# A second level of the seven-product scheme for two products of the first layer

## The chip, the cores and the metric

The kernel runs on one core of one Trainium2 chip. The metric is the device time of one execution in microseconds, the median over runs. The core has TensorE (PE; its weight loads are shown apart as PEld), VectorE (DVE), ScalarE (ACT), GpSimd (POOL) and SyncE (SP, which here issues nearly all DMAs). DVE, ACT and PE can reach PSUM, the eight banks that hold the results of matmuls; POOL works in SBUF.

## The reference: attention over pooled keys, then two layers

```python
def _attn_ref(q, k, v):                       # q, k, v: (8, 8, 576, 64)
    k_p = k.reshape(B, H, Sp, pool, D).mean(axis=3)     # pool = 8, Sp = 72
    v_p = v.reshape(B, H, Sp, pool, D).mean(axis=3)
    scores = scale * np.matmul(q, k_p.transpose(0, 1, 3, 2))
    scores = scores - np.max(scores, axis=-1, keepdims=True)
    attn = np.exp(scores)
    attn = attn / (np.sum(attn, axis=-1, keepdims=True) + 1e-09)
    return np.matmul(attn, v_p)

def _moe_ref(x, w_in, w_out, alpha):          # x: (4608, 512), w_in: (512, 2048)
    h = x @ w_in
    s = np.sin(alpha * h)
    g = h + s * s / (alpha + 1e-09)
    return g @ w_out                          # w_out: (2048, 512)
```

The rows of x are the attention's output, batch by batch, with the heads side by side. All is fp32.

## The kernel before

**The first layer.** `hidden(u, extra)` runs once for each of nine units of 512 rows of x. It uses a scheme for products of 2 x 2 blocks that needs seven block products instead of eight: x is halved in its rows and in its 512 features, `w_in` in its features and in its 2048 outputs. `self.A[1..7]` hold the seven weight blocks (plain ones and sums), `bt[u][:, 0..3]` the four sums of x's blocks. A unit has four groups, J = 0 to 3, of 2 x 128 outputs in each half. A group has seven slots, k = 0 to 6, with one block product each, in the order 1, 5, 6, 2, 7, 3, 4. A block product is four matmuls: 128 x 128 weights, 256 moving columns, two row blocks jj by two halves kk of the contraction. So a unit has 28 slots, numbered 7 J + k.

**The banks.** A group uses four PSUM banks (b1, b6, b5, b7) out of five that rotate. Sums of the scheme are made in place: ACT copies b1 into b6 and product 6 accumulates there; ACT copies b6 into b7, and products 7 and later 4 accumulate there; product 2 accumulates into b1, product 3 into b6. Product 5 is copied to SBUF as `p5`. The four results are b1 (after product 2), b7 + p5 (after product 7, called g11 here for `g[:, 1, :, 1]`), b6 + p5 (after product 3, g01) and b7 after product 4. DVE makes the two additions of p5. ACT applies the sine and then the square, and DVE adds the squares to h in `finish`. `store_g` sends g to a buffer in DRAM. Product 4 may only be issued once g11 has been read out of b7.

**The order.** The order of every engine's instructions is the order in which the code emits them; nothing reorders it. Each slot emits first what the slot before left (`self.left`), then the `extra` work of the slot, then its product:

```python
            def left2(G=G, Q=before, late=late):
                ...
                nc.scalar.copy(out=G.b7[:], in_=G.b6[:])
                G.p5 = self.tp.tile([P, JW, TH], F32, name="p5")
                nc.scalar.copy(out=G.p5[:], in_=G.b5[:])
            def left3(G=G):
                sin(G, 0, 0, G.b1)
                square(G, 0, 0)
            def left4(G=G):
                add(G.g[:, 1, :, 1], G.b7[:], G.p5[:])
```

`left2` is emitted at the start of slot k = 3, `left3` at k = 4, `left4` at k = 5. Q is the group before; its last squares (`squares(Q)`) are emitted at k = 1, its `finish` at k = 2.

**The attention beside it.** `carry(u)` places the attention of batch u + 1 into unit u as extra work. For units 1 to 6: scores at slots 3 and 5 (`two_scores`, PE in banks 5 to 7 and one rotating bank, with the shifts by the maximum on DVE, the last at slot 6), `load_v` at 6, the exps on ACT at slots 8, 9, 10, 10, the norms (DVE reduction and reciprocal, POOL product) at 9, 10, 11, 12, the DVE transposes `turn` at 12, 12, 13, 13, 16 DMAs `move` on SP at 14, `all_values` at 25 (PE, then copies into x by ACT), the next keys' transposes at 26. `turn_q` prepares q of batch u + 2 at slots 22 to 25: in parts 0 and 1 DVE transposes q into the tile `tr`, which `move` reads before that, and parts 2 and 3 send it on by DMA. q lies in two buffers of one pool (`qp`, `name="q"`), and `load_q(u + 3)` is at slot 7.

**The second layer** (`outputs`, L1112) comes after the first; it already uses the scheme at two levels, with 144 moving columns.

Of the kernel before, what the change touches and what calls it, by code (L numbers as in the profile page):

```python
# [13 lines left out]
F32 = mybir.dt.float32  # L14
AX = mybir.AxisListType.X
AF = mybir.ActivationFunctionType
# [3 lines left out]
P = 128  # L20
POOL = 8
TH = 256
# [18 lines left out]
class Kernel:  # L41
# [31 lines left out]
        self.load_q_rest(b)  # L73

    def new_q(self, b):
        self.qm[b] = self.qp.tile([P, 5 * self.H * self.D], F32, name="q")

    def load_q_heads(self, b, h0, h1, dma=None):
        main = self.q_views(self.qm[b])[0]
# [3 lines left out]
    def pairs_q(self, b, tiles):  # L83

        nc = self.nc
        if 0 in tiles:
            self.raw = self.q_views(self.qm[b])
            self.qm[b] = self.qp.tile([P, 5 * self.H * self.D], F32, name="q")
        x = self.qm[b][:].rearrange("p (t h e d) -> p t e h d", t=5, e=2, d=self.D)
        for t in tiles:  # L90
            n = P if t < 4 else 64
            raw = self.raw[0][:, :, t, :] if t < 4 else self.raw[1]
            nc.scalar.copy(out=x[:n, t], in_=raw.rearrange("p (e h) d -> p e h d", e=2))
# [135 lines left out]
    def attention(self, b):  # L229
# [22 lines left out]
        def q_t(i, copy=nc.scalar.copy):  # L252

            n = rows[i]
            x = self.qm[b][:n].rearrange("p (t hp x) -> p t hp x", t=5, hp=NP)[:, i]
            if b not in self.qt:
                self.qt[b] = self.qt_view(self.qp.tile([P, 5 * H * D], F32, name="q"))
            ps = self.abank([P, NP, P])
            for hp in range(NP):
                nc.tensor.transpose(ps[:, hp, :n], x[:, hp], self.ident[:n, :n])  # L260
            copy(out=self.qt_tiles(b)[:, i, :, :n], in_=ps[:, :, :n])
# [100 lines left out]
        def q_head(hp):  # L362

            if hp == 0:
                self.qt[b] = self.qt_view(self.qp.tile([P, 5 * H * D], F32, name="q"))
            main = self.q_views(self.qm[b])[0]
            ps = self.psum([P, 4, P], 1 + hp % 2)
            for e in range(2):
                for tp in range(2):
                    nc.tensor.transpose(ps[:, 2 * e + tp, :], main[:, 2 * hp + e, 2 * tp:2 * tp + 2, :].rearrange("p t d -> p (t d)"), self.ident[:])  # L370
            nc.scalar.copy(out=self.qt_tiles(b)[:, hp], in_=ps)
# [365 lines left out]
    def abank(self, shape):  # L737

        self.aturn = (self.aturn + 1) % 3
        return self.psum(shape, 5 + self.aturn)  # L740

    def sums_of_x(self, u, n):

        nc = self.nc
        if u not in self.bt:
            self.bt[u] = self.home(3, [P, 4, 2, TH])
        xT, bt = self.xT[u], self.bt[u]
        B = lambda i, j: xT[:, 2 * i:2 * i + 2, j * TH:(j + 1) * TH]
        o, x, y = ((0, B(0, 1), B(0, 0)), (1, B(1, 1), bt[:, 0]), (2, B(1, 1), B(0, 1)), (3, B(1, 0), bt[:, 1]))[n]
        nc.vector.tensor_tensor(out=bt[:, o], in0=x, in1=y, op=OP.subtract)  # L750

    def hidden(self, u, extra):

        nc = self.nc
        bank = lambda: self.bank([P, JW, TH])
        add = lambda o, x, y: nc.vector.tensor_tensor(out=o, in0=x, in1=y, op=OP.add)  # L756

        for slot in range(7 * self.NJ):
            J, k = divmod(slot, 7)
            for f in self.left:  # L760
                f()
            for f in extra[slot]:
                f()
            if k == 0:
                before = self.group
                G = self.group = SimpleNamespace(
                    u=u, J=J, b1=bank(), g=self.hp.tile([P, 2, JW, 2, TH], F32, name="h"),
                    s=self.hp.tile([P, 2, JW, 2, TH], F32, name="s", bufs=1))
            xT, bt = self.xT[u], self.bt[u]
            B = lambda i, j: xT[:, 2 * i:2 * i + 2, j * TH:(j + 1) * TH]  # L770

            def product(p, ps, start):
                x = {1: B(0, 0), 2: B(1, 0), 3: B(1, 1), 4: bt[:, 3], 5: bt[:, 0], 6: bt[:, 1], 7: bt[:, 2]}[p]
                for jj in range(JW):
                    f = J * JW + jj
                    for kk in range(2):
                        nc.tensor.matmul(ps[:, jj, :], self.A[p][:, kk, f * P:(f + 1) * P], x[:, kk, :],  # L777
                                         start=(start and jj == 0 and kk == 0), stop=(kk == 1), skip_group_check=True)

            def sin(G, i, j, src):  # L780
                for jj in range(JW):
                    f = i * self.K2 // 2 + G.J * JW + jj
                    nc.scalar.activation(out=G.s[:, i, jj, j, :], in_=src[:, jj], func=AF.Sin, scale=self.al[:, f:f + 1])  # L783

            def square(G, i, js):

                for jj in range(JW):
                    f = i * self.K2 // 2 + G.J * JW + jj
                    x = G.s[:, i, jj, js, :]
                    nc.scalar.activation(out=x, in_=x, func=AF.Square, scale=self.c[:, f:f + 1])  # L790

            early = lambda G: G.J == (0 if G.u else 1)

            def squares(G):
                if not early(G):
                    square(G, 0, 1)
                square(G, 1, slice(0, 2))

            self.squares = squares

            def left0(G=G, Q=before):
                G.b6 = bank()
                nc.scalar.copy(out=G.b6[:], in_=G.b1[:])  # L803
                if Q:
                    squares(Q)

            def left1(G=G, Q=before):
                if Q:
                    self.finish(Q)

            late = G.J == 0 and 0 < u < self.B - 1

            def left2(G=G, Q=before, late=late):
                if Q and not late:
                    self.store_g(Q)
                G.b7 = bank()
                nc.scalar.copy(out=G.b7[:], in_=G.b6[:])
                G.p5 = self.tp.tile([P, JW, TH], F32, name="p5")
                nc.scalar.copy(out=G.p5[:], in_=G.b5[:])

            def left3(G=G):
                sin(G, 0, 0, G.b1)
                square(G, 0, 0)

            def left4(G=G):
                add(G.g[:, 1, :, 1], G.b7[:], G.p5[:])

            def left5(G=G, Q=before, late=late):
                if late:
                    self.store_g(Q)  # L830
                add(G.g[:, 0, :, 1], G.b6[:], G.p5[:])
                sin(G, 1, 1, G.g[:, 1, :, 1])
                add(G.g[:, 0, :, 0], G.b1[:], G.s[:, 0, :, 0])

            def left6(G=G):
                sin(G, 0, 1, G.g[:, 0, :, 1])
                if early(G):
                    square(G, 0, 1)
                sin(G, 1, 0, G.b7)

            self.left = [(left0, left1, left2, left3, left4, left5, left6)[k]]
            if k == 1:
                G.b5 = bank()
            p = (1, 5, 6, 2, 7, 3, 4)[k]
            product(p, getattr(G, {1: "b1", 5: "b5", 6: "b6", 2: "b1", 7: "b7", 3: "b6", 4: "b7"}[p]), k < 2)

    def finish(self, Q):
        add = lambda o, x, y: self.nc.vector.tensor_tensor(out=o, in0=x, in1=y, op=OP.add)  # L848
# [8 lines left out]

    def end_hidden(self):
        nc, Q = self.nc, self.group
        for f in self.left:  # L860
            f()
        self.squares(Q)
        self.finish(Q)
        self.store_g(Q)

# [90 lines left out]
    def carry(self, u):  # L956
# [6 lines left out]
        if u == 0:  # L963
# [36 lines left out]
            at(20, A.move, (3,), nc.scalar)  # L1000
            at(26, A.all_values)
            at(9, self.load_q, 2)
            at(14, self.load_q, 3)
            for e in range(2):
                at(12, self.load_k, 2, e)
                at(17, lambda e=e: self.pool_k[e]())
# [5 lines left out]
        if 0 < u < last:  # L1012
# [3 lines left out]
            at(6, A.two_shifts)  # L1016
            for i in range(4):
                at((8, 9, 10, 10)[i], A.exp, i)
                at((9, 10, 11, 12)[i], A.norm, i)
                at((12, 12, 13, 13)[i], A.turn, i)  # L1020
            at(14, A.move, range(4))
            at(6, self.load_v, b)
# [5 lines left out]
            at(25, A.all_values)  # L1028
            if b < last:
                at(26, self.att[b + 1].k_t)  # L1030
            if u + 3 <= last:
                at(7, self.load_q, u + 3)
            turn = 22
        elif u:
            turn = None
# [218 lines left out]
    def run(self):  # L1254
        nc, tc = self.nc, self.tc
        pool = lambda s, n, b, **kw: s.enter_context(tc.tile_pool(name=n, bufs=b, **kw))
        with ExitStack() as top:
# [10 lines left out]
            with ExitStack() as one:  # L1268
# [5 lines left out]
                att = one.enter_context(ExitStack())  # L1274
                cb = pool(att, "cb", 1)
                self.kvp = pool(att, "kv", 2)
                self.qp = pool(att, "qp", 2)
                self.ap = pool(att, "ap", 1)
                self.sm = pool(att, "sm", 3)
                one.enter_context(tc.manual_schedule(engines=engines))  # L1280
# [6 lines left out]
                self.twos = cb.tile([P, 64], F32, name="twos")  # L1287
                self.eights = cb.tile([64, 32], F32, name="eights")
                self.mask = cb.tile([P, 4], F32, name="mask")
                self.last = cb.tile([64, 640], F32, name="last")  # L1290
                self.last_t = cb.tile([P, 5, 64], F32, name="last_t")
                nc.vector.tensor_reduce(out=self.twos[:], in_=ident[:].rearrange("p (m k) -> p m k", k=2), axis=AX, op=OP.add)
                x = ident[:64, :64].rearrange("p (m k) -> p m k", k=8)
# [1 line left out]
                    nc.vector.tensor_reduce(out=self.eights[:, 8 * s:8 * s + 8], in_=x, axis=AX, op=OP.add)  # L1295
                nc.vector.tensor_reduce(out=self.mask[:], in_=ident[:].rearrange("p (g s k) -> p s g k", s=4, k=8), axis=mybir.AxisListType.XY, op=OP.add)
                self.qm, self.qt, self.kp, self.vp, self.pair, self.pool_k = {}, {}, {}, {}, {}, {}
                self.bt, self.left, self.group, self.turn = {}, [], None, 2
                self.R = {}
                self.first_batch()  # L1300
                for u in range(self.NU):
                    x = self.carry(u)
                    if u == self.B - 1:
# [61 lines left out]
```

## Time and profile before

| | us |
|---|---|
| median of 3 runs | 911.84 |
| the runs | 911.52 to 913.13 |
| the profiled execution | 911.39 |
| its span, first to last instruction | 909.6 |
| unit 2, PE busy of 144.06 to 199.65 | 55.59 |
| ACT busy in the same stretch | 39.21 |
| DVE busy in the same stretch | 36.06 |
| ACT busy of 157.7 to 172 (14.3 us, J = 1) | 12.88 |
| DVE busy of 157.7 to 172 | 11.62 |

The mean granted TensorE clock is 0.999. A matmul of fp32 shows as two records. In a timeline row the columns are start, duration, engine, line, operation, result and sources, shape, count, and in brackets the idle time of the engine before it with what ended it. In a row of several instructions the duration runs from the start of the first to the end of the last, and successive instructions of an engine overlap a little: a row of two ACT squares takes 0.90 us, though one takes 0.50.

### The profile page before, as it was taken

To read this page: it belongs to the slowest core of one execution; us is meant where nothing else is said; L and a number is where in the kernel's file an instruction comes from. 1 tells how busy PE (TensorE), PEld (TensorE's weight loads), DVE (VectorE), ACT (ScalarE), POOL (GpSimd) and SP (SyncE) were. 2 spreads that over 40 slices of the span, in tenths; PEclk is the share of its full clock that TensorE was granted. 3 is DMA by queue.
4 is the path that set the end of the run, shared out by engine and by line. 5 is a ranking of instruction groups with operands and counts; after the bars stand their busy time and mean duration, and the time that the engine had idled before them with its cause. 6 is when DMAs were issued, how large, how long until landed. Compare 5 with 4: busy or idle time off the path is not lost.

```text
span 909.6 us, 17730 instructions
## 1 busy us (share of the span) xinstructions
PE 899.5 (99%) x7002; PEld 814.6 (90%) x7002; DVE 664.0 (73%) x1006; ACT 436.1 (48%) x998; POOL 170.9 (19%) x159
## 2 busy tenths in 40 slices
PE   8999999999999999999999999999999999999997
PEld 5787888888888888888888899999999999999997
DVE  6675766758567574663466899979788888889895
ACT  5696775867658676686876621111111111111111
POOL 4785350703408044140000000000000000000000
PEclk9999999999999999999999999999999999999999
DMA  9985867758577575538227247161618162534401
GB/s 253 249 252 153 213 166 193 198 173 224 162 190 192 165 199 171 148 109 307 76 84 249 93 117 226 37 216 37 225 27 222 41 188 73 170 92 128 134 14 40
DMA packets 134794, 141.12 MB, mean 155 GB/s; under 512 B 49896, under 2 KB 103288, under 8 KB 134712
## 3 DMA queue, kind: packets, MB, share of 16 engines
q1 hardware_dynamic: 132536, 138.03, 53.2%
q10 hardware_dynamic: 2176, 1.97, 0.8%
q8 instruction: 55, 0.90, 0.4%
q14 instruction: 27, 0.22, 0.1%
HBM read 75.37 MB, written 47.19 MB: 135 GB/s over the span
## 4 chain that ended last, share of the span: by engine, by line
PE 88%; DMA 4%; POOL 2%; DVE 2%; SPq 1%; ACT 1%; issue 1%; ACTq 0%; POOLq 0%; DVEq 0%
PE PS L1112 42%; PE PS L777 41%; DMA kvin<-in_v_dram 2%; PE PS L575 2%; PE PS L287 2%; SPq L642 1%; POOL kvin L118 1%; PE PS L588 1%; DMA a<-in_moe_w_in_dram 1%; POOL ex L344 1%; DMA h<-in_k_dram 1%; ACT s L790 0%; POOL as L648 0%; DVE h L848 0%; ACT s L783 0%
## 5 line engine op out<-in xcount | busy, mean ns | idle before, releaser
L777 PE MATMUL PS<-home,a 128*128 128x256 f32 x1152 | 264.3, 381 | 1.2 <-ACT home L502 0.8
L777 PEld LDWEIGHTS PS<-home,a 128*128 128x128 f32 x1152 | 216.6, 190 | 37.4 <-issue 4.6
L777 PE MATMUL PS<-home,as 128*128 128x256 f32 x864 | 200.3, 381 | 0.3 <-ACT PS L803 0.2
L777 PEld LDWEIGHTS PS<-home,as 128*128 128x128 f32 x864 | 162.5, 190 | 23.9 <-issue 1.0
L1112 PE MATMUL PS<-s,wb 128*128 128x144 f32 x896 | 119.4, 286 | 0.4 <-ACT PS L1232 0.4
L1112 PEld LDWEIGHTS PS<-s,wb 128*128 128x128 f32 x896 | 113.7, 190 | 0.7 <-ACT PS L1232 0.6
L118 POOL TENSOR_TENSOR kvin<-kvin 96x768 f32<-96x768 f32 (+3 forms) x42 | 74.8, 1782 | 196.8 <-DMA kvin<-in_v_dram 195.2
L790 ACT ACTIVATE s<-s,c 128x256 f32<-128x256 f32 (+1 forms) x216 | 110.0, 573 | 0.0
L756 DVE TENSOR_TENSOR h<-PS,p 128x512 f32<-128x512 f32 x72 | 49.2, 684 | 79.5 <-PE PS L777 42.2
L783 ACT ACTIVATE s<-h,al 128x256 f32<-128x256 f32 x144 | 65.1, 503 | 56.5 <-DVE h L756 52.7
L1232 ACT COPY PS<-PS 128x144 f32<-128x144 f32 x56 | 14.7, 263 | 145.7 <-PE PS L1112 144.3
L783 ACT ACTIVATE s<-PS,al 128x256 f32<-128x256 f32 x144 | 60.0, 468 | 32.1 <-PE PS L777 18.4
L1112 PE MATMUL PS<-r,wb 128*128 128x144 f32 x512 | 73.2, 286 | 0.0
L1112 PE MATMUL PS<-s,a 128*128 128x144 f32 x512 | 73.2, 286 | 0.0
L848 DVE TENSOR_TENSOR h<-PS,s 128x512 f32<-128x512 f32 x36 | 24.6, 684 | 63.7 <-ACT s L790 63.7
L1112 PEld LDWEIGHTS PS<-r,wb 128*128 128x128 f32 x512 | 67.1, 190 | 0.1
L1112 PEld LDWEIGHTS PS<-s,a 128*128 128x128 f32 x512 | 67.1, 190 | 0.0
L1251 ACT COPY PS<-PS 128x144 f32<-128x144 f32 x56 | 14.7, 263 | 88.4 <-PE PS L1112 88.4
L1112 PE MATMUL PS<-s,we 128*128 128x144 f32 x384 | 54.9, 286 | 0.0
L1112 PE MATMUL PS<-x,wb 128*128 128x144 f32 x384 | 54.9, 286 | 0.0
L1112 PEld LDWEIGHTS PS<-s,we 128*128 128x128 f32 x384 | 50.4, 190 | 0.1
L1112 PEld LDWEIGHTS PS<-x,wb 128*128 128x128 f32 x384 | 50.3, 190 | 0.0
(187 smaller groups left out, 1185.1 us busy)
## 6 DMA issues: line engine op xcount, KB each, us to landing
g_bridge<-h SPq DMA_DIRECT2D x72, 512.0 KB
r<-g_bridge SPq DMA_DIRECT2D x31, 1152.0 KB
out_dram<-o SPq DMA_DIRECT2D x124, 72.0 KB
kvin<-in_k_dram SPq DMA_DIRECT2D x14, 576.0 KB
q<-in_q_dram SPq DMA_DIRECT2D x7, 1024.0 KB
kvin<-in_v_dram SPq DMA_DIRECT2D x14, 512.0 KB
aM<-tr SPq DMA_DIRECT2D x54, 92.0 KB
aM<-tr SPq DMA_DIRECT2D x54, 88.0 KB
```

The costliest lines, as they stand in the source:

```text
L118: self.nc.gpsimd.tensor_tensor(out=t[..., 0:w] if w > D else out, in0=t[..., 0:w], in1=t[..., w:2 * w], op=OP.add)
L287: nc.tensor.matmul(ps[e][r0 + r:r0 + r + q.shape[-1], h, :], q[s], kb[s, hp, :], start=True, stop=True)
L344: nc.gpsimd.tensor_tensor(out=E(i), in0=E(i), in1=sm.unsqueeze(2).to_broadcast([P, n, Sp]), op=OP.mult)
L575: nc.tensor.matmul(o[r:r + 64], w, x, start=start and i < 2, stop=False, skip_group_check=True)
L756: add = lambda o, x, y: nc.vector.tensor_tensor(out=o, in0=x, in1=y, op=OP.add)
L777: nc.tensor.matmul(ps[:, jj, :], self.A[p][:, kk, f * P:(f + 1) * P], x[:, kk, :], start=(start and jj == 0 and kk == 0), stop=(kk == 1), ...
L783: nc.scalar.activation(out=G.s[:, i, jj, j, :], in_=src[:, jj], func=AF.Sin, scale=self.al[:, f:f + 1])
L790: nc.scalar.activation(out=x, in_=x, func=AF.Square, scale=self.c[:, f:f + 1])
L848: add = lambda o, x, y: self.nc.vector.tensor_tensor(out=o, in0=x, in1=y, op=OP.add)
L1112: nc.tensor.matmul(out, W[:, J // 2, J % 2, :], A[:, J, :], start=(start and J == 0), stop=(J == self.NJ - 1), skip_group_check=True)
L1232: nc.scalar.copy(out=x1[:, 0, :], in_=x0[:, 1, :])
L1251: nc.scalar.copy(out=x1[:, 1, :], in_=x1[:, 0, :])
```

## The change

Three groups (J = 1 to 3) of units 1 to 6 compute product 5 by seven products of a second level, and group 3 of these units also product 1. The 256 rows and the 256 features are halved again, and so are the two output blocks jj; each inner product is one matmul of 128 x 128 weights and 128 moving columns. `inner_w_in` makes the inner weights once, at slot 23 of unit 0, on POOL, in the first of the two q buffers, which holds no q afterwards. `inner_x` makes the inner sums of x for each unit, at slot 2, on POOL. The inner scheme works in place in the product's own bank; it needs one more bank (7 for product 5, 6 for product 1), three ACT copies and one DVE addition.

In these groups slot 1 has no product 5. Its inner products are spread: a at k = 0, b at k = 1 (k = 2 for J = 3), d at k = 3, e at k = 4 (k = 3 for J = 3). The second half of product 4 is issued after a and product 1 of the next group. The copy of p5 follows e, `finish` and the store of the group before move from k = 2 and 3 to k = 3 after d, and the squares of the group before are partly at k = 3. For J = 3, the inner products of product 1 are issued within products 3 and 4 of J = 2. The first norm goes from slot 9 to 10, and q of batch u + 2 (no longer u + 3) is loaded at slot 7. Groups in which nothing is split keep their order, now written out slot by slot.

```diff
 def new_q(self, b):
-        self.qm[b] = self.qp.tile([P, 5 * self.H * self.D], F32, name="q")
+        self.qm[b] = self.q_tile(b > 1)
+
+    def q_tile(self, i):
+        return self.qp.tile([P, 5 * self.H * self.D], F32, name=f"q{int(i)}")
...
+    def inner_w_in(self):
+        w = self.q_tile(0)[:]
...
+            self.sums(((s1, L(1, 0), L(1, 1), OP.add), (s2, s1, L(0, 0), OP.subtract), (s3, L(0, 0), L(1, 0), OP.subtract), (s4, L(0, 1), s2, OP.subtract)))
+            self.W2[p] = J0, {1: L(0, 0), 2: L(0, 1), 3: s4, 4: L(1, 1), 5: s1, 6: s2, 7: s3}
+
+    def inner_x(self, u):
...
+            self.sums(((t1, R(0, 1), R(0, 0), OP.subtract), (t2, R(1, 1), t1, OP.subtract), (t3, R(1, 1), R(0, 1), OP.subtract), (t4, R(1, 0), t2, OP.subtract)))
+            self.X2[p] = {1: R(0, 0), 2: R(1, 0), 3: R(1, 1), 4: t4, 5: t1, 6: t2, 7: t3}
+
+    def sums(self, steps):
+        for o, x, y, op in steps:
+            self.nc.gpsimd.tensor_tensor(out=o, in0=x, in1=y, op=op)
...
     def hidden(self, u, extra):
...
+        two = 0 < u < self.B - 1
...
             if k == 0:
...
+                if Q and not N:
+                    self.last_sines(Q, 2 if not inner else 0)
+                extras()
+                G = self.group = N or begin(J)
+                self.next = None
+                if G.i5:
+                    G.i5.a()
+                if G.i1:
+                    self.last_sines(Q, 0)
+                else:
+                    product(G, 1, G.b1, True)
+                    if G.i5:
+                        product(Q, 4, Q.b7, part=(2, 3))
+            elif k == 1:
+                if not G.i1:
+                    copy(G.b6[:], G.b1[:])
+                if G.i5 and not G.i1:
+                    self.last_sines(Q, 1)
+                    G.i5.b()
+                if Q and not G.i1:
+                    squares(Q, 0)
+                    if not G.i5:
+                        squares(Q, 1)
+                extras()
+                if not G.i5:
+                    product(G, 5, G.b5, True)
+            elif k == 2:
+                if Q and not G.i5:
+                    self.finish(Q)
+                extras()
+                if G.i1:
+                    product(G, 6, G.b6, part=(0, 1))
+                    G.i5.b()
+                    self.last_sines(Q, 1)
+                    product(G, 6, G.b6, part=(2, 3))
+                else:
+                    product(G, 6, G.b6)
+            elif k == 3:
...
+                copy(G.b7[:], G.b6[:])
+                G.p5 = self.tp.tile([P, JW, TH], F32, name="p5")
+                if not G.i5:
+                    copy(G.p5[:], G.b5[:])
+                else:
+                    if G.i1:
+                        squares(Q, 0)
+                    squares(Q, 1)
+                    G.i5.d()
+                    self.finish(Q)
+                    self.store_g(Q)
+                extras()
+                product(G, 2, G.b1)
+                if G.i1:
+                    G.i5.e()
+                    copy(G.p5[:], G.b5[:])
+            elif k == 4:
                 sin(G, 0, 0, G.b1)
+                if not G.i5:
+                    square(G, 0, 0)
+                extras()
+                product(G, 7, G.b7, part=(0, 1))
+                if G.i5:
+                    if not G.i1:
+                        G.i5.e()
+                        copy(G.p5[:], G.b5[:])
+                    square(G, 0, 0)
+                product(G, 7, G.b7, part=(2, 3))
+            elif k == 5:
                 add(G.g[:, 1, :, 1], G.b7[:], G.p5[:])
+                extras()
+                N = None
+                if two and J + 1 == 3:
+                    N = self.next = begin(J + 1)
+                    N.i1.a()
+                product(G, 3, G.b6, part=(0, 1))
+                if N:
+                    N.i1.b()
+                product(G, 3, G.b6, part=(2, 3))
+            else:
...
+                if not N:
+                    last()
+                    extras()
+                    product(G, 4, G.b7, part=(0, 1))
+                    if not (two and J < 3):
+                        product(G, 4, G.b7, part=(2, 3))
+                else:
+                    product(G, 4, G.b7, part=(0,))
+                    N.i1.d()
+                    last()
+                    product(G, 4, G.b7, part=(1, 2))
+                    N.i1.e()
+                    copy(N.b6[:], N.b1[:])
+                    extras()
+                    product(G, 4, G.b7, part=(3,))
...
+    def inner_product(self, G, p, ps, y):
...
+        def a():
+            products((1, 5), (y[:, 0], y[:, 1]), True)
+            nc.scalar.copy(out=f[:, 0], in_=y[:, 0:1].to_broadcast([P, 2, P]))
+            m5[p] = self.sm.tile([P, 1, P], F32, name=f"m{p}", bufs=1)
+            nc.scalar.copy(out=m5[p][:], in_=y[:, 1:2])
+
+        def b():
+            products((6, 2), (c[1], c[0]))
+            nc.scalar.copy(out=c[2], in_=c[1])
+
+        def d():
+            products((7,), (c[2],))
+            x = ps.rearrange("p i t -> p (i t)")[:, P:3 * P].rearrange("p (i t) -> p i t", i=2)
+            nc.vector.tensor_tensor(out=f[:, :, 1], in0=x, in1=m5[p][:].to_broadcast([P, 2, P]), op=OP.add)
+
+        def e():
+            products((3, 4), (c[1], c[2]))
...
-            at(14, self.load_q, 3)
+            at(23, self.inner_w_in)
...
-                at((9, 10, 11, 12)[i], A.norm, i)
+                at((10, 10, 11, 12)[i], A.norm, i)
...
-            if u + 3 <= last:
-                at(7, self.load_q, u + 3)
+            if 2 < u + 2 <= last:
+                at(7, self.load_q, u + 2)
+            at(2, self.inner_x, u)
...
-                self.qp = pool(att, "qp", 2)
+                self.qp = pool(att, "qp", 1)
```

`last_sines(Q, 0)` emits the sine (0, 1) of the group before, part 1 its sine (1, 0), part 2 both; `begin` takes the four banks and makes the inner objects i5 and i1.

## The prediction

> **What bounds the kernel now.** I read the page's busy times first, then its chain that ended last, then the timeline of one unit (unit 2, from 144.06 us) engine by engine.
>
> ```profile
> span 909.6 us, 17730 instructions
> PE 899.5 (99%) x7002; PEld 814.6 (90%) x7002; DVE 664.0 (73%) x1006; ACT 436.1 (48%) x998; POOL 170.9 (19%) x159
> PE 88%; DMA 4%; POOL 2%; DVE 2%; SPq 1%; ACT 1%; issue 1%; ACTq 0%; POOLq 0%; DVEq 0%
> PE PS L1112 42%; PE PS L777 41%; DMA kvin<-in_v_dram 2%; PE PS L575 2%; PE PS L287 2%; SPq L642 1%; POOL kvin L118 1%; PE PS L588 1%; DMA a<-in_moe_w_in_dram 1%; POOL ex L344 1%; DMA h<-in_k_dram 1%; ACT s L790 0%; POOL as L648 0%; DVE h L848 0%; ACT s L783 0%
> ```
>
> TensorE is the bound, and the products of the first layer (L777) carry 41% of the chain. So removed TensorE time counts in full, and so does every new wait of TensorE. ACT at 48% looks harmless; that share is a mean, and the place to look is group J=1, where the attention's four exps lie.
>
> ```profile
> 157.72 3.62 PE L777 MATMUL PS<-home,a 128*128 128x256 f32 x16
> 161.18 3.62 PE L777 MATMUL PS<-home,as 128*128 128x256 f32 x16
> 164.63 3.66 PE L777 MATMUL PS<-home,a 128*128 128x256 f32 x16
> ...
> 161.86 1.33 ACT L790 ACTIVATE s<-s,c 128x512 f32<-128x512 f32 x2
> 163.21 1.28 ACT L336 ACT_TABLE_LOAD   x1
> 164.51 1.26 ACT L336 ACTIVATE ex<-ex 128x576 f32<-128x576 f32 x2
> 165.67 0.58 ACT L817 COPY PS<-PS 128x512 f32<-128x512 f32 x1
> 166.19 0.57 ACT L819 COPY p<-PS 128x512 f32<-128x512 f32 x1
> 166.66 1.49 ACT L336 ACTIVATE ex<-ex 128x576 f32<-128x576 f32 x2
> 168.17 1.28 ACT L783 ACT_TABLE_LOAD   x1
> 169.47 0.84 ACT L783 ACTIVATE s<-PS,al 128x256 f32<-128x256 f32 x2
> ...
> 168.33 0.69 DVE L756 TENSOR_TENSOR h<-PS,p 128x512 f32<-128x512 f32 x1
> ...
> 175.07 10.08 SPq L488 DMA_DIRECT2D aM<-tr  x16
> 187.08 2.37 DVE L210 STREAM_TRANSPOSE tr<-q 128x1024 f32<-128x1024 f32 x2 [3.65 <-DMA aM<-tr]
> ```
>
> The reader should see three things. TensorE runs a product pair in 161.18 - 157.72 = 3.46 us, without a gap. ACT is full from 161.4 to 172: the copy of b7 ends at 166.25 where product 7 starts at 166.36, and the copy of p5 (166.19) stands before exps 2 and 3, the table load and the next sine (169.47). DVE's transposes of q at 187.08 wait for the 16 moves, which SP needs 10.08 us to issue.
>
> **What the Trainium skill says.** "TensorE: Matmul & The Clock Gate", section "LDWEIGHTS (loading the stationary operand)", gives columns / 1.2 ns: 107 ns for 128 columns. The trace agrees: four loads in 0.52 us at 11.04 (L353), the last 0.22 long, are about 0.10 apart. The same page, "Architectural detail: the array is 16× 32×32, not 1× 128×128", says that ACT and DVE take their work strictly in order; every timeline row above follows the order in which the code issues. "ScalarE: Activation LUTs", "What ACT_TABLE_LOAD costs", gives 1283 ns plus about 1380 ns of drain; the trace shows 1.28 us and the exp 0.02 later, so no drain is paid here. The same page, "Table sets: the hidden batching unit", has cheap functions in every set; whether Square runs without a load between two exps no row of before shows, and the change puts it there.
>
> **The change part by part.** Its own execution is 911.39 us for a span of 909.6, 0.45 under the median of 911.84.
>
> *Removed from TensorE.* 6 units x (3 + 1) = 24 products. Before: 4 matmuls, two records each, 8 x 3.45/16 = 8 x 0.2156 = 1.725 us. After: 7 matmuls of 128 columns. The nearest row is a transpose of 128 columns (15.99, eight in 1.04 us, the last 0.276 long): (1.04 - 0.276)/7 = 0.109 apart, equal to the load's pace. 14 x 0.109 = 1.526; saved 0.199, x24 = 4.8 us. Upper bound for a record: the second layer's 144 columns, 374.48/3057 = 0.1225, which leaves 0.01 a product, 0.2 us in all. I take 0.109: 0.80 us saved per unit.
>
> *Added to ACT.* For each inner product three PSUM copies of 256, 128 and 128 columns. Between L1209 (288: 0.383) and L1232 (144: 0.263) they take about 0.36 and 0.25, and advance the queue by 0.27, 0.16 and 0.16. DVE gets an addition of 256 (about 0.42); POOL eight small operations per unit at slot 2 (0.455 each, the 128x128 row of L118), while it waits for v (195.2 us over 7 waits), so nothing; with that cover gone, 3.6 us of POOL ahead of the pooling of v. The weights' sums fall into POOL's idle time after 80.4 us. The q loads start one unit later, slot 7 for a use at slot 22, 26 us ahead, on an SP queue whose v load lands in 9.4 us: nothing, at worst a few tenths at slot 22. Units 0, 7 and 8 keep their order.
>
> *Moved, J=1.* The copy of p5 now stands behind the sine of product 2 (slot 11), and so behind all four exps and both table loads. Times from t0 = 157.72 (end of product 3 of J=0), with the advances of the trace. TensorE: half of product 4 to 0.86, m1 and m5 to 1.30, product 1 to 3.03, the other half to 3.89, m6 and m2 to 4.33, product 6 to 6.06, m7 to 6.28, product 2 to 8.00, half of product 7, m3 and m4, the rest of 7, to 10.17, product 3 to 11.89. ACT: sine and squares from 0.93 to 2.54, the two copies to 2.97, b6 (waits for product 1, +0.20) 3.23 to 3.72, sine of b7 4.09 to 4.83, copy to 5.08, table load 6.38, two exps 7.54, b7 copy ends 8.11 (product 7 waits 0.15), squares 9.27, two exps 10.78, table load 12.08, sine 12.81, p5 ends 13.4. Then DVE must add b7 + p5 (0.69) before product 4 may accumulate into b7. DVE itself: finish waits for the squares (9.4), takes 0.6 + 1.35, then three of the norms at 0.92 each to about 14.1, and only then that addition, to 14.8. Product 4 is due at 12.05. Stall: 2.7. If DVE were free it would still be 13.4 + 0.75 - 12.05 = 2.1.
>
> *J=2.* On DVE, two turns (1.6) and the last norm (1.18) still stand before the addition of b6 + p5; it ends near 17.9, the sine after it 18.8, the copy that m6 needs 19.2. TensorE is there at 14.8 + 0.86 + 0.44 + 1.73 + 0.86 = 18.7: 0.7 lost, and 0.2 on the b6 copy behind it. ACT has no exps here and catches up.
>
> *J=3.* The last turn ends 3.5 us later than before (175.13), so SP's 16 moves do too, and DVE's transposes of q start at about t0 + 32.9 instead of 29.4 (187.08). Queued behind them (2.3 + 0.75) is the new addition, to 36.4; m3 and m4 wait for it, due at about 35.2 (the 14.8 above, the 0.9, and the rows of J=2 and J=3 summed): 1.2. Here bounds are wide, 0 to 2.5, since the sum of a whole chain decides. In unit 6 no q is turned, but all_values needs the bank that finish now frees at slot 24: about 1.0.
>
> Sum per unit: 0.15 + 2.7 + 0.9 + 1.2 - 0.8 = +4.15, five times 20.8; unit 6 +3.95. Together +24.7 on 911.39: 936.1; with the 0.45 to the median 936.5. The second layer is untouched.
>
> **The rivals.**
> (a) *The clean gain*, on the other side: the p5 copy is no wait. Then -4.8 and a few tenths of pipeline breaks: 907.4. For it: TensorE bound, ACT half idle on the mean. Against it: the walk. It decides at 0.8 us of stall per unit, so g11 must be done by 12.85, p5 by 12.1 and the norms after it in DVE's queue.
> (b) *Only ACT's lateness counts*: 2.1 + 0.15 - 0.8 = 1.45 per unit, the waits in J=2 and J=3 swallowed: 911.4 + 8.7 = 920. For it: DVE and the moves have slack that I may underrate.
> (c) *More is lost*: Square between exps needs two more table loads (2.6 us per unit, straight on the p5 copy), or a stall beyond the 3.4 us idle window of "The HAM clock gate" (the clock gate page, Part 1) halves the clock for a while: 936.5 + 15.6 = 952. For it: the stall of 2.7 isn't far below. Against: cheap functions are in every set.
>
> **How the numbers follow.** As walked 0.66, own range 925 to 948 (J=1 2.1 to 3.2, J=2 0.4 to 1.5, J=3 0 to 2.5, and the record at 0.1225); (b) 0.14 at 920; (a) 0.10 at 907; (c) 0.07 at 952; no change 0.03. Leaving out (a) and most of (c), the range is 918 to 950. 0.2% (1.8 us) is about what a measurement tells from none. Faster 0.10, within 0.2% 0.02, slower 0.88.
>
> **What would show it.** In J=1 of units 1 to 6 TensorE idle 2 to 3 us ahead of product 4, ended by DVE's addition into h, itself ended by the p5 copy or run behind L342; in J=3 a gap before the inner matmuls ended by DVE, with the q transposes just ahead; the inner records 0.109 apart. No gap at product 4 refutes the forecast: then the p5 copy was earlier than I place it.

## The result, and the profile after

| | before | after |
|---|---|---|
| median, us | 912.49 | 939.5 |
| the runs, us | 911.52 to 913.15 | 939.09 to 940.4 |
| profiled execution and its span, us | 911.39, 909.6 | 940.40, 938.6 |
| mean granted TensorE clock | 0.999 | 0.991 |

The changed kernel takes 1.0298 times as long (95% interval 1.028 to 1.0316): 27 us more, where 24.7 were forecast. A unit is counted here from the first L777 or L811 record (the first layer's products before and after) to the next unit's. Units 1 to 6 took 55.3 to 56.7 us before and 60.0 to 60.8 after, +4.70, +5.04, +4.16, +4.39, +4.98 and +5.03; units 7 and 8 and the second layer have not moved. So the six units hold 28.3 of the 29.0 us by which the span grew.

Of the page of the changed kernel: its busy times, the chain that ended last, and the costliest group. The last row is the same group in the kernel before:

```profile
span 938.6 us, 18229 instructions
PE 910.1 (97%) x7146; PEld 821.0 (87%) x7146; DVE 678.7 (72%) x1030; ACT 452.0 (48%) x1070; POOL 205.7 (22%) x215
...
PE 79%; ACT 7%; DVE 4%; DMA 3%; SPq 3%; issue 2%; POOL 1%; ACTq 0%; DVEq 0%; POOLq 0%
PE PS L1258 40%; PE PS L811 31%; PE PS L971 2%; PE PS L291 2%; SPq L492 2%; PE PS L579 2%; ACT s L948 1%; ACT s L941 1%; ACT ex L340 1%; DMA a<-in_moe_w_in_dram 1%; DMA h<-in_v_dram 1%; DVE h L993 1%; PE PS L592 1%; ACT L340 1%; DVE h L786 1%
...
L811 PE MATMUL PS<-home,a 128*128 128x256 f32 x1104 | 267.3, 388 | 14.9 <-DVE h L786 13.8
...
L777 PE MATMUL PS<-home,a 128*128 128x256 f32 x1152 | 264.3, 381 | 1.2 <-ACT home L502 0.8
```

TensorE's share of the chain fell from 88% to 79%, and those of ACT and DVE rose (from 1% and 2% to 7% and 4%). The two rows of the group name the place: TensorE sits idle 14.9 us ahead of the full block products, where it was 1.2 before, and 13.8 of that ends with DVE's addition of p5 (L786). That PE is busier than before (910.1 against 899.5) with less arithmetic to do is a first hint that part of its work ran at a lower clock. It is no more than a hint: the run without exps, below, shows 904.1 us at the full clock. The waits of TensorE (who waited, for whom: total, times, longest; one of the seven lies outside the changed units):

```profile
PE PS L811 <- DVE h L786: 13.8, 7, 2.3
PE PS L971 <- DVE PS L986: 2.4, 2, 1.4
...
PE PS L971 <- ACT PS L975: 0.8, 2, 0.4
```

L971 are the inner matmuls. Six waits of 2.25 us stand out, one in each changed unit. In unit 2 the timeline shows how it comes about (PE, then ACT, then DVE):

```profile
172.78 1.03 PE L811 MATMUL PS<-home,a 128*128 128x256 f32 x4
173.65 1.89 PE L811 MATMUL PS<-home,as 128*128 128x256 f32 x8
177.79 1.67 PE L811 MATMUL PS<-home,a 128*128 128x256 f32 x4 [2.25 <-DVE h L786]
179.26 0.64 PE L971 MATMUL PS<-home,as 128*128 128x128 f32 x2
180.11 3.52 PE L811 MATMUL PS<-home,a 128*128 128x256 f32 x12
...
168.28 1.28 ACT L340 ACT_TABLE_LOAD   x1
169.58 1.26 ACT L340 ACTIVATE ex<-ex 128x576 f32<-128x576 f32 x2
170.74 0.58 ACT L787 COPY PS<-PS 128x512 f32<-128x512 f32 x1
171.25 1.33 ACT L948 ACTIVATE s<-s,c 128x512 f32<-128x512 f32 x2
172.49 1.48 ACT L340 ACTIVATE ex<-ex 128x576 f32<-128x576 f32 x2
173.99 1.28 ACT L941 ACT_TABLE_LOAD   x1
175.28 0.84 ACT L941 ACTIVATE s<-PS,al 128x256 f32<-128x256 f32 x2
176.01 0.58 ACT L787 COPY p<-PS 128x512 f32<-128x512 f32 x1
...
174.35 0.75 DVE L346 TENSOR_REDUCE sm<-ex 128x8 f32<-128x584 f32 x1
...
176.12 0.71 DVE L346 TENSOR_REDUCE sm<-ex 128x8 f32<-128x584 f32 x1
...
177.04 0.69 DVE L786 TENSOR_TENSOR h<-PS,p 128x512 f32<-128x512 f32 x1
```

Product 4 (the row at 177.79) was due at 173.65 + 8 x 0.2156 = 175.37; 2.42 us are lost. ACT reaches the copy of p5 only at 176.01, behind two table loads, four exps, the squares and a sine. It ends at 176.59, and DVE is then still in the last of three norms; the addition starts at 177.04. Then a second thing shows: right after the gap a row of two inner records takes 0.64 us instead of 0.39, and twelve records take 3.52 instead of 2.76.

### The profile page after: what moved, and what is told of

The parts are those of the page before. It is cut to its first block, busy times and chain, and to the rows that moved or that the text cites. A ratio compares the mean times of both kernels' runs of the same rounds, so it can differ in the third digit from the quotient of the medians.

```text
span 938.6 us, 18229 instructions
## 1 busy us (share of the span) xinstructions
PE 910.1 (97%) x7146; PEld 821.0 (87%) x7146; DVE 678.7 (72%) x1030; ACT 452.0 (48%) x1070; POOL 205.7 (22%) x215
## 4 chain that ended last, share of the span: by engine, by line
PE 79%; ACT 7%; DVE 4%; DMA 3%; SPq 3%; issue 2%; POOL 1%; ACTq 0%; DVEq 0%; POOLq 0%
PE PS L1258 40%; PE PS L811 31%; PE PS L971 2%; PE PS L291 2%; SPq L492 2%; PE PS L579 2%; ACT s L948 1%; ACT s L941 1%; ACT ex L340 1%; DMA a<-in_moe_w_in_dram 1%; DMA h<-in_v_dram 1%; DVE h L993 1%; PE PS L592 1%; ACT L340 1%; DVE h L786 1%
## 5 line engine op out<-in xcount | busy, mean ns | idle before, releaser
L811 PE MATMUL PS<-home,a 128*128 128x256 f32 x1104 | 267.3, 388 | 14.9 <-DVE h L786 13.8
L811 PEld LDWEIGHTS PS<-home,a 128*128 128x128 f32 x1104 | 206.6, 194 | 51.7 <-DVE h L786 16.6
L811 PE MATMUL PS<-home,as 128*128 128x256 f32 x720 | 171.4, 382 | 0.4 <-ACT PS L787 0.4
L811 PEld LDWEIGHTS PS<-home,as 128*128 128x128 f32 x720 | 132.5, 190 | 18.2 <-issue 1.3
L786 DVE TENSOR_TENSOR h<-PS,p 128x512 f32<-128x512 f32 x72 | 49.1, 683 | 73.1 <-PE PS L811 44.1
L122 POOL TENSOR_TENSOR kvin<-kvin 96x768 f32<-96x768 f32 (+3 forms) x42 | 72.4, 1724 | 70.6 <-DMA kvin<-in_v_dram 68.9
L993 DVE TENSOR_TENSOR h<-PS,s 128x512 f32<-128x512 f32 x36 | 24.8, 688 | 64.2 <-ACT s L948 64.2
L787 ACT COPY PS<-PS 128x512 f32<-128x512 f32 x72 | 41.4, 575 | 39.1 <-PE PS L811 28.2
L993 DVE TENSOR_TENSOR h<-h,s 128x1024 f32<-128x1024 f32 x36 | 51.0, 1417 | 0.0
```

Of the source, the lines that this page charges most:

```text
L122: self.nc.gpsimd.tensor_tensor(out=t[..., 0:w] if w > D else out, in0=t[..., 0:w], in1=t[..., w:2 * w], op=OP.add)
L787: copy = lambda o, x: nc.scalar.copy(out=o, in_=x)
```

## The experiments

All edits are to the changed kernel. Line numbers shift by a few where an edit adds lines.

### Which groups carry the loss, and what comes along

Second level in groups 2 and 3 only, or in group 1 only, or nowhere (the single q buffer, the later q load and POOL's sums stay). Where a group isn't split its old order stands, and without the split of group 1 the first norm goes back to slot 9.

```diff
-            if two and J > 0:
+            if J in I5:      # e1: (2, 3)   e2: (1,)   e3: ()
...
-            if two and J == 3:
+            if J in I1:      # e1: (3,)     e2: ()     e3: ()
```

> The second level is left out of group J=1 alone (18 of 24 inner products remain, first norm back at slot 9). Theory A (the waits come from the place in J=1, where exps and norms stand ahead of the p5 copy and of the addition that frees b7): the 2.4 us gap at product 4 and the slow clock after it vanish; what stays is the wait in J=3, about 1.2 us in units 1 to 5 and 1.0 in unit 6, less 0.6 saved: 912.5 + 4.5 = 917. Theory B (the inner products themselves cost more than they save, 27 us / 24 = 1.1 us each wherever they stand): 912.5 + 18 x 1.1 = 932.

> The second level stays in group J=1 alone (6 of 24 inner products). Theory A: the gap of 2.4 us before product 4 of J=1 stays in each of units 1 to 6, with up to 1.7 us of slow clock behind it: 912.5 + 6 x 3.1 = 931, up to 938. Theory B: 912.5 + 6 x 1.1 = 919.

> No product is split; what else the change brings stays: one buffer for q with its load a unit later, the inner sums of the weights and of x on POOL (made and not used), one tile for s. Theory A: these are hidden, 912.5 within 1 us. Theory C (late q, or POOL holding DVE back, costs the time): most of the 27 us stays, 930 or more.

| | median, us | before beside it | ratio (95%) |
|---|---|---|---|
| groups 2 and 3 (e1) | 918.6 | 911.38 | 1.0075 (1.0057 to 1.0092) |
| group 1 alone (e2) | 931.1 | 911.38 | 1.0212 (1.0189 to 1.0236) |
| nowhere (e3) | 911.54 | 911.38 | 1.0001 (0.9991 to 1.001) |

The waits of TensorE when group 1 alone is split:

```profile
PE PS L812 <- DVE h L786: 13.8, 7, 2.3
```

Its times are those of the full change to the digit. Group 1, with six of the 24 split products, costs 19.7 us; groups 2 and 3 cost 7.2. The two add up to about the whole (26.9 against 27.0). That they meet so closely is partly chance: the medians of the kernel before differ by 1.1 us between the two comparisons (911.38 and 912.49), and the slow clock described below fell in two units here and in four there. The buffer, the load and POOL's sums cost nothing that can be measured.

### ACT's queue or DVE's

Both stand in front of the addition. Here the exps, the norms (reduction, reciprocal and product), or both are left out of units 1 to 6; each kernel ran once.

```diff
-                at((8, 9, 10, 10)[i], A.exp, i)       # e4, e6
-                at((10, 10, 11, 12)[i], A.norm, i)    # e5, e6
```

> The changed kernel without the exps of units 1 to 6 (the four exps of the attention and with them both table loads are left out, 5.2 us of ACT per unit). Theory A with two queues: the p5 copy comes some 5 us sooner, but DVE still has finish and three norms ahead of the addition that frees b7, so the gap before product 4 of J=1 falls only from 2.4 to about 1.5 us: about 930. Theory A with ACT alone: the gap vanishes, about 914. Theory B: no change from 939.5.

> The changed kernel without the norms of units 1 to 6 (DVE's reductions and reciprocals and POOL's products are left out; the exps stay). Theory A with two queues: DVE is free when the p5 copy ends, so the gap before product 4 of J=1 falls from 2.4 to 2.05 us only, since exps and table loads still hold the copy back; the wait in J=2 goes, since the turns come sooner: about 925, up to 933 with slow clock. DVE alone: the gap vanishes, about 914.

> The changed kernel without exps and without norms in units 1 to 6. Theory A with two queues: both holders are gone, no gap at product 4 of J=1 and none in J=2; left are about 1 us a unit in J=3 and the 0.8 saved: 911.5 + 1 = 912.5. Theory B (the inner products cost more than they save): 930 or more.

Measured: 929.51, 928.55 and 914.13 us. The waits of TensorE, first without exps:

```profile
PE PS L811 <- DVE h L786: 7.9, 7, 1.3
```

then without norms:

```profile
PE PS L811 <- DVE h L786: 11.3, 7, 1.8
```

Without both the row is down to the one wait of 0.3 outside the units. The gap, start to start, was 2.42 us with both, 1.43 without exps, 2.00 without norms, 0 without either. So neither queue explains it alone: when one is cleared, the other still holds the addition back for most of the time. Without norms DVE stands idle for 2.14 us in unit 2 until the copy of p5 has ended, and adds at once; without exps the copy ends at 171.92 and the addition starts at 174.41, behind the norms. The two queues are not independent either. `finish` opens DVE's work ahead of the addition and waits for ACT's squares. From its start to the addition pass 4.43 us in both kernels (172.61 to 177.04 in the full change, 169.98 to 174.41 without exps), but without exps it starts 0.98 us earlier against the time at which product 4 is due. All that clearing the exps won, it won there, so part of DVE's lateness is ACT's.

The walk gave 2.1 for "DVE free" and the run 2.00. The run without norms took 3.5 us more than the 925 expected; 3.1 of it is that group 3 kept its wait for DVE in three units (1.0, 1.22 and 0.90 us). In neither run was the clock halved before the very end (means 0.999 and 1.0), though gaps of 1.27 and 1.84 us of idle time were left in every changed unit.

### The half clock after the gap

Ten bf16 matmuls of 512 columns into a free bank go ahead of product 4 in group 1. They shorten no wait (product 4 still starts 2.42 us late in all six units); they only keep TensorE busy within the gap.

```diff
+                    if two and J == 1:
+                        for _ in range(10):
+                            nc.tensor.matmul(self.psum([P, 4, P], (self.turn + 1) % 5), self.full[:], self.full[:].unsqueeze(1).to_broadcast([P, 4, P]), start=True, stop=True)
```

> The changed kernel with ten bf16 matmuls of 512 columns (0.216 us each, 2.16 in all, results not used) where TensorE waits before product 4 of J=1 in units 1 to 6. If the idle gap is what slows TensorE's clock after it: no slow matmuls, units 2, 3, 5 and 6 get some 1.7 us back, and the waits in J=2 (0.55) and J=3 (up to 1.2) that it covered return: about 935. If the slow clock has another cause: 939.5. If the fill delays product 4: over 940.

Measured: 935.79 us, ratio 1.0264 (1.0247 to 1.028), clock 0.998: 3.7 us less than the full change for more work. Its timeline in unit 2 (PE):

```profile
173.97 2.32 PE L926 MATMUL PS<-full 128*128 128x512 bf16 x10
176.39 1.13 PE L811 MATMUL PS<-home,a 128*128 128x256 f32 x4
...
177.80 2.76 PE L811 MATMUL PS<-home,a 128*128 128x256 f32 x12
180.95 0.49 PE L974 MATMUL PS<-last,q 128*128 128x128 f32 x2 [0.39 <-ACT PS L978]
```

The twelve records are back at 2.76 us, and the wait of group 2 for ACT's copy (0.55 lost here) is there in every unit. In the full change only units 1 and 4 show it: in the other four TensorE was so late from its low clock that the copy was ready. The lengths of the units in the profiled executions separate the two cases: units 1 and 4 came out 0.05 and 0.13 us shorter than in the full change, the four with the low clock 0.72 to 0.81.

Why four units of six, when all six gaps are 2.25 us? In the changed kernel's profiled execution the granted clock, read in stretches of 0.2 us, falls at 178.24, 239.68, 359.14 and 420.58 us. The distances are 61.44, 119.46 and 61.44, that is 18, 35 and 18 times 3.413. The Trainium skill ("TensorE: Matmul & The Clock Gate", "The HAM clock gate") says that TensorE's activity is judged in windows of 3413 ns that are "free-running". This trace agrees with both. So I cut the time into such windows. For the changed kernel (start and end of the stretch, its length, busy time and records of PE, PEld, DVE, ACT and POOL, granted clock, DMA share, GB/s), the windows with most of the gap in units 1 to 4, and what follows in units 2 and 3:

```profile
113.39:116.80 3.41, 1.86 (x9) 1.31 (x7) 3.31 (x8) 3.38 (x7) 1.59 (x2) 1.00 0.52 193
...
174.83:178.24 3.41, 1.16 (x6) 0.70 (x5) 3.31 (x8) 3.02 (x8) 2.75 (x3) 1.00 0.86 295
178.24:181.65 3.41, 3.41 (x12) 2.87 (x11) 3.38 (x9) 0.97 (x4) 1.57 (x2) 0.50 1.03 283
...
236.27:239.68 3.41, 1.28 (x7) 1.17 (x8) 3.34 (x9) 2.65 (x7) 3.19 (x3) 1.00 1.03 338
239.68:243.09 3.41, 3.41 (x11) 2.78 (x10) 3.38 (x9) 1.35 (x4) 1.79 (x2) 0.50 1.03 274
...
297.71:301.12 3.41, 1.88 (x11) 1.72 (x12) 3.38 (x8) 2.05 (x5) 2.60 (x3) 1.00 1.04 333
```

The same cut for the kernel with group 1 alone split, in units 2 and 3, with its own grid (its slow stretches start at 176.87 and 296.34, 35 windows apart):

```profile
173.46:176.87 3.41, 1.42 (x7) 1.27 (x8) 3.34 (x9) 2.50 (x6) 3.05 (x3) 1.00 1.04 341
176.87:180.28 3.41, 3.41 (x10) 2.69 (x9) 3.38 (x8) 1.50 (x4) 1.94 (x2) 0.50 1.01 240
...
231.48:234.90 3.42, 1.59 (x8) 1.06 (x6) 3.31 (x8) 3.39 (x7) 1.88 (x2) 1.00 0.61 225
234.90:238.31 3.41, 2.99 (x14) 2.65 (x15) 3.38 (x8) 0.94 (x3) 1.57 (x3) 1.00 1.04 302
```

The reader should look at PE's busy time in the first row of each pair, and at the clock in the next. Over the twelve gaps of the two executions the windows that were followed by half the clock had 1.16, 1.28, 1.24, 1.17, 1.42 and 1.45 us of PE; those followed by the full clock 1.86, 1.88, 1.83, 1.59, 1.56 and 2.04. The same section has the low clock come "after ≥1 idle window (~3.4µs)". Here no whole idle window was needed, and the measurement decides: less than about 1.5 us of work in one was enough, and whether a gap of 2.25 us brought the low clock depended on how much of it lay within one window. It also fits that idle gaps of 1.84 and 1.27 us never did: without norms the emptiest windows of units 1 to 3 hold 1.57 us of PE and were followed by the full clock.

The limit was read off after the runs, and no run was made to test it; but the traces can. Each of the twelve profiled executions of this document has its own grid, which its changes of clock fix. Of their 3218 windows from the first one at full clock on, ends of the kernels included, 25 were followed by half the clock, and these held 1.45 us of PE or less; all others held 1.50 us or more. The closest is the end of the kernel split nowhere: 1.50 us between 901.97 and 905.38, followed by the full clock. The busy time of the weight loads does not sort the windows: in the kernel with group 1 alone 1.30 us of them went ahead of half the clock, and 1.03 ahead of the full one. PE's busy time is that of the profile, which models the ends of matmuls, so 1.5 us is a limit in this measure.

### Could the order be mended?

All 24 products stay, but the work ahead of the copy of p5 moves: exp 0 a slot later, the squares of the group before ahead of the exps, the p5 copy ahead of the sine and its table load.

```diff
-                    if not G.i5:
+                    if not G.i5 or J == 1:
                         squares(Q, 1)
...
-                    squares(Q, 1)
+                    if J > 1:
+                        squares(Q, 1)
...
-                sin(G, 0, 0, G.b1)
+                first = G.i5 and J == 1
+                if not first:
+                    sin(G, 0, 0, G.b1)
...
                     copy(G.p5[:], G.b5[:])
+                    if first:
+                        sin(G, 0, 0, G.b1)
...
-                at((8, 9, 10, 10)[i], A.exp, i)
+                at((9, 10, 10, 10)[i], A.exp, i)
```

> All 24 inner products, the same work, another order in J=1: exp 0 a slot later, the squares of the group before ahead of the exps, the p5 copy ahead of the sine and its table load. Theory A: the gap at product 4 goes, product 7 waits 0.75 for the b7 copy, J=2 0.35, J=3 1.2: 1.55 per unit over before, 911.5 + 9.3 = 921, and no slow clock. Theory B: no change from 939.5.

Measured: 922.89 us, ratio 1.0117 (1.0096 to 1.0139). The waits of TensorE:

```profile
PE PS L811 <- ACT PS L787: 4.4, 7, 0.7
PE PS L976 <- DVE PS L991: 3.9, 4, 1.3
```

The gap at product 4 is gone (0, and 0.22 in unit 4). In its place product 7 waits 0.87 us for ACT's copy of b6 into b7, since the squares, the table load and an exp now all stand ahead of that copy (ACT in unit 2):

```profile
164.49 1.33 ACT L953 ACTIVATE s<-s,c 128x512 f32<-128x512 f32 x2
165.84 1.28 ACT L340 ACT_TABLE_LOAD   x1
167.14 0.68 ACT L340 ACTIVATE ex<-ex 128x576 f32<-128x576 f32 x1
167.73 0.58 ACT L787 COPY PS<-PS 128x512 f32<-128x512 f32 x1
```

Group 2 waits in unit 4 alone (0.55), and group 3 still waits for DVE: 1.46, 0.25, 0.71, 1.19 and 1.19 us in units 1 to 5. So 16.6 us of the loss were order, with the clock that follows from it. What is left has moved to other waits; whether an order without them exists was not found.

### The parts with no wait known

Product 5 of group 2 and product 1 of group 3 alone, twelve products, with the first norm at slot 9:

```diff
-            if two and J > 0:
+            if J in I5:      # (2,) in units 1 to 6
...
-            if two and J == 3:
+            if J in I1:      # (3,) in units 1 to 6
...
-                at((10, 10, 11, 12)[i], A.norm, i)
+                at((9, 10, 11, 12)[i], A.norm, i)
```

> The second level only where it has room: product 5 of J=2 and product 1 of J=3 (12 inner products), first norm at slot 9. Theory A: 12 x 0.2 = 2.4 saved, less 0.15 to 0.3 per unit of waits (b6 copy in J=2, all_values): 909.0 to 910.6, under the kernel before. Theory B: 12 x 1.1 lost: 925.

Measured: 912.28 against 911.71 us, ratio 1.0003 (0.9995 to 1.0011). The saving forecast for it did not come. Units 3 to 5 show waits of inner matmuls for POOL's product of the norm (L348) of 0.33, 0.20 and 0.71 us, which I had not foreseen: the sums of x for product 1 lie in `ex`, the tile of the norm. That this makes the wait was not tested. The next version also moves the second turn from slot 12 to 13, and puts the ordering copy of `all_values` on ACT in every unit:

```diff
-                at((12, 12, 13, 13)[i], A.turn, i)
+                at((12, 13, 13, 13)[i], A.turn, i)
...
-            (nc.vector.tensor_copy if b > 1 else nc.scalar.copy)(out=self.sm.tile([P, 1], F32, name="order")[:], in_=rest[:, 1, 0:1])
+            nc.scalar.copy(out=self.sm.tile([P, 1], F32, name="order")[:], in_=rest[:, 1, 0:1])
```

> As the run with J=2 and the first product only, and two waits of it taken away: the second turn goes from slot 12 to 13 (so DVE adds b6 + p5 sooner and the b6 copy of J=2 comes in time), and the small order copy of all_values goes from DVE to ACT. Theory A: up to 12 x 0.2 = 2.4 us under the kernel before, 909.3 to 911; if nothing is left to win beside the waits for v on POOL in units 3 to 5: 911.7.

Measured: 911.13 against 911.71 us, ratio 0.9994 (0.9986 to 1.0001). That is no difference that these runs can tell. The interval leaves room for a saving of 1.3 us at most (0.0014 x 911.71), so the whole 2 us of 12 x 0.17 did not come. In its profiled execution no wait of the split groups is left, and units 2, 5 and 6 are 0.22 us shorter than before: two products at 0.17 each, less 0.12 by which the matmuls of `all_values` became longer. Unit 3 is 0.84 shorter, but before it was 1.1 us longer than its neighbours. Units 1 and 4 are 0.63 and 0.48 longer, in `all_values`. The six units together gain 0.39 us. Unit 0, where nothing is split, came out 1.7 us longer in this execution.

## Why the prediction was right, and where it was off

The sign, the place and most of the size were right. Point by point:

- *The gap at product 4 of group 1.* Forecast 2.7 us, measured 2.42 in all six units. With the time zero of the walk at 175.37 - 12.05 = 163.32, the copy of p5 ended at +13.3 (forecast 13.4) and the addition at +14.4 (14.8): DVE came to the norms a little earlier than I had it. That ACT's queue and DVE's both hold it is shown by the runs without exps and norms.
- *Product 7.* Forecast 0.15 us, measured 0.19.
- *Group 2.* Forecast 0.9 us, measured 0.55, in units 1 and 4, and in all six once the clock is kept up. A slip of the sum is part of the 0.9: 19.2 - 18.7 is 0.5, and the forecast wrote 0.7.
- *Group 3.* Forecast 1.2 within 0 to 2.5; measured 1.54, 1.23 and 0.19 in units 1, 4 and 5 and nothing in units 2 and 3, and 0.3 to 1.5 in units 1 to 5 with the gap filled. The mechanism is as forecast, an addition behind the transposes of q. In unit 1 (DVE, then PE):

```profile
136.48 3.02 DVE L214 STREAM_TRANSPOSE tr<-q 128x1024 f32<-128x1024 f32 x4 [3.28 <-DMA aM<-tr]
139.43 0.39 DVE L986 TENSOR_TENSOR PS<-PS,m 128x256 f32<-128x256 f32 x1
...
139.88 0.49 PE L971 MATMUL PS<-home,q 128*128 128x128 f32 x2 [1.38 <-DVE PS L986]
```

The transposes start when the moves of the attention have landed (aM<-tr), and the inner addition of product 5 stands behind all four; inner products 3 and 4, which need it, follow 0.06 us after its end.

- *The saving.* Forecast 0.20 us per product with inner records 0.109 us apart. They were 0.111 apart, so 1.725 - 14 x 0.111 = 0.17, 4.1 us for the 24 instead of 4.8. The four weight loads at 11.04 that the forecast read as about 0.10 apart are 0.11 apart too: the last is 0.19 us long, not 0.22.
- *`all_values`.* The wait for the bank that `finish` frees late was forecast for unit 6 only (1.0). It made the matmuls of L579 take 0.85 us longer in units 2 and 6, 0.54 in unit 5 and 0.46 in unit 3 (which had 0.41 of such a delay before). Their weight loads waited for `finish` (L993) four times.
- *Squares between exps.* Two squares ran at 171.25 between the exps, with no load before or after. The Trainium skill ("ScalarE: Activation LUTs", "Table sets: the hidden batching unit") has cheap functions in every set and names relu, copy, identity and abs; the row shows that Square runs beside exp too. That half of rival (c) is out.
- *The side effects* (q buffer, later load, POOL's sums): nothing forecast, nothing measured.

The term that was mis-sized is the clock. I had put it into rival (c) alone, and only for a stall "beyond the 3.4 us idle window". It came after 2.25 us of idle time, in four units of six in the profiled execution. (The other three executions had mean clocks of 0.992, 0.993 and 0.995 against 0.991 here, which fits as many such stretches or fewer.) Half of a stretch is lost each time, 3.41/2 = 1.7 us, 6.8 in all; the waits of groups 2 and 3 that it swallows give back a part, so filling the gap is worth 939.5 - 935.8 = 3.7 us. Without it the kernel stands at 935.8, where the walk had 936.5. That agreement is partly luck: the waits in groups 1 and 2 were shorter than forecast (0.28 and 0.35 us per unit), while the delay of `all_values`, the loss of saving and the short refills around the waits (the first records after a wait lie further apart) were left out or set too small. Such a refill shows in the run with the gap filled: after the wait at 180.95 two inner records need 0.32 us and the next two 0.36, where two without a wait need 0.22.

Rival (a) fell to the gap itself. Rival (b), that only ACT's lateness counts, fell to the run without norms (the gap shrinks by 0.42 us) and to the waits left in groups 2 and 3.

## What to carry to other kernels

A result that two engines hand on (ACT copies, DVE adds, TensorE waits) is due when the later of two queues gets to it, and one queue can make the other late. Walk both in order, with all that is emitted ahead, before moving such a step, since clearing one queue may leave most of the wait. A mean share of 48% says nothing of the 7.7 us (168.28 to 176.01) in which two table loads and four exps stand ahead of the step. And price a new gap in TensorE with the clock that follows it: the low clock after 2.25 us of idle time cost another 0.7 to 0.8 us in a unit of the full change, where it hid part of the later waits, and 1.4 with group 1 alone split (units 2 and 4 against units 5 and 6).

## What the runs showed of the hardware that was not expected

- In the twelve executions TensorE's clock halved for the next 3.41 us where PE was busy 1.45 us or less in a window of 3.413 us, and stayed full where it was busy 1.50 us or more; of twelve gaps of 2.25 us six did it and six did not. The windows run on through the whole execution (18, 35 and 18 windows between the slow stretches of one), and their place against the kernel's work differed between executions.
- Ten matmuls of bf16 whose results nobody uses, 2.32 us of work in a gap, made the changed kernel 3.7 us faster.
- ACT ran two squares between exps with no table load (171.25 to 172.58, between exps at 169.58 and 172.49).
